# K and V in one load each, and the scores, P, b1 and wo that go with it, in a one-token attention and MLP kernel

## The chip, the core and the metric

The kernel runs on one core of a Trainium2 chip. A core has TensorE (PE, matmuls), VectorE (DVE), ScalarE (ACT), GpSimd (POOL), SyncE (SP, which here only issues transfers) and 16 DMA engines that carry all transfers between HBM and SBUF. The metric is the device time of one execution in microseconds; lower is better.

## The reference

One token of width 1024 goes through two branches that are added to it. The weights and the two caches, 39.85 MB in all, are read once.

```python
xn = layernorm(x)                                   # x: 1 x 1024
# A: attention of one token over the last W = 4096 keys
q = (xn @ wq).reshape(32, 128)                      # wq: 1024 x 4096; 32 heads
k, v = k_cache[:, -W:], v_cache[:, -W:]             # 4 groups x 4096 x 128, 8 heads share a group
p = softmax(q @ k.T * 128**-0.5)
a = (p @ v).reshape(4096) @ wo                      # wo: 4096 x 1024
# B: an MLP
y = layernorm(xn)
b = gelu(y @ w1 + b1) @ w2 + b2                     # w1: 1024 x 3584, w2: 3584 x 1024
out = x + a + b
```

## The kernel before

**Order.** Every engine runs one list of instructions, written out by hand, with semaphore waits between engines. What sets the order of the big transfers is SP's list, one queue: the first half of wq (rows 0 to 3 of 8 per partition), the first K load, the second half of wq, the second K load, all of W1; then, after a wait for the last K transpose (`C["kt", 3]`, since V overwrites K in the tile `KV`), two V loads (L313); after a wait for q's last matmul (`done["q"]`), W2 in 16 and 12 rows per partition (it overwrites wq in `BIG`); after a wait for W1's last matmul (`done["h"]`), wo in 8, 12, 9, 2 and 1 rows per partition (L320). Of wo, 20 rows go to `BIG` behind W2 and 12 to `KT`. x, b2 and b1 are loaded by ACT's queue at the start; b1 is laid out as 128 partitions of 28 numbers.

**K and V.** `pairs(cache, c)` describes one load, that of groups 2c and 2c+1 (L228). The memory side is walked as 64 rows m, within each 2 groups g, within each 64 keys of 128 numbers (16 KB that lie in one piece). On the SBUF side these are 128 partitions, so partition 2m + g holds 64 keys of one group and neighbouring partitions hold different groups:

```python
return cache[0, 2 * c:2 * c + 2, SK - W:SK, :].rearrange("g (m i) d -> m g (i d)", m=64)
```

**Attention.** DVE turns K in four transposes of 4096 columns (L285, `turn_k`, in blocks of 32 x 32), three of them ahead of q's own transpose and one behind. q (64 matmuls, weights streamed against a zero-padded x, `XZ`) is copied out, turned and spread into `QBD`. PE adds a mask into four PSUM banks (L455: -1e30 where a column's key belongs to the other group than the row's) and then 32 score matmuls of 512 columns. DVE takes two maxima, brings them together across partitions, ACT takes the exponential of 2048 columns with its sum, DVE turns P in one transpose into `PT` (L350), and after W1's product PE does 32 matmuls of `PT` with V (L433, two groups of 256 columns). DVE divides by the sum and picks each row's part, and four small matmuls (`pe_turn_o`, L513) turn the result. These are done after four of the W2 rounds.

**MLP and end.** W1's product is 56 matmuls into one bank; four small matmuls (L494) turn it, DVE adds b1 and does the GELU. W2 and the first 20 rows of wo are multiplied in 12 rounds of four rows (`pe_round`), each after POOL has raised `s_feed` for its rows' landing. The last 12 rows of wo are multiplied in four column strips of 32 PSUM partitions each as they land (L433, 128 x 256 pieces), ACT and DVE evict bank 7 (L400), SP writes the output as two rows of 512.

All matmuls that add into a bank go through the helper `add`, so they share line L433 in the profile and are told apart by their tiles: `BIG,XZ` is q, `KT,QBD` scores, `BIG,YZ` W1, `KV,KT` P times V, `BIG,GO` the rounds, `KT,GO` the last rows.

## Time and profile before

| | us |
|---|---|
| median of 3 runs | 99.3 (99.14 to 99.41) |
| the profiled execution | 99.2 |
| its span in the profile | 97.6 |
| PE, DVE, ACT, POOL busy | 71.6, 37.9, 8.1, 10.2 |
| DMA queue q1, share of 16 engines' span | 95.7% |
| K lands (second load), W1 lands, wo lands | 32.4, 49.3, 95.5 |
| last K transpose ends, V issued | 42.9, 42.9 |
| scores, W1's product, P times V end | 48.2, 62.1, 72.0 |

Times are from the span's start. A group's row gives line, engine, operation, tiles written and read, count; behind the first bar busy time and the mean of one in ns; behind the second the idle time of the engine just before and what ended it. In the chain, "DMA BIG<-in_B_w_dram 47%" is the share of the span in which the end waited for that transfer. Issue rows have KB per transfer and the median time from issue to landing; a transfer queued behind others has a long one. The slice rows give tenths busy in 40 equal slices of the span.

### The profile page before, as it was taken

How to read it: one execution, taken by the hardware profiler on the slowest of the kernel's cores; microseconds unless marked ns; L12 is line 12 of the kernel's file. 1: busy time of each engine (PE TensorE's matmuls, PEld its weight loads, DVE VectorE, ACT ScalarE, POOL GpSimd, SP SyncE). 2: the span in 40 equal slices, each digit the busy share in tenths (PEclk: the TensorE clock that was granted, in tenths of full speed). 3: DMA queues.
4: the chain of work that ended last, by engine and by line, in shares of the span. 5: the costliest groups of instructions: out<-in, count | busy, mean ns of one | idle time of the engine just before them, and what ended most of it. 6: DMA issues, size and time to landing. Idle time of an engine off the chain costs nothing.

```text
span 97.6 us, 1259 instructions
## 1 busy us (share of the span) xinstructions
PE 71.6 (73%) x337; PEld 30.1 (31%) x349; DVE 37.9 (39%) x50; ACT 8.1 (8%) x16; POOL 10.2 (10%) x29
## 2 busy tenths in 40 slices
PE   0005000399999973879979999799989999997991
PEld 0001000033444320323334444333344444443450
DVE  0001899899930699950581800050043000000001
ACT  0500000600000023000008000200000010000001
POOL 6999600000000000000000000000000000000000
PEclk9999999999999999999999999999999999999999
DMA  7599999999999998888999999999899998999980
GB/s 215 228 431 444 410 432 437 430 430 443 417 430 464 682 400 376 376 376 376 430 437 430 437 497 443 443 430 400 373 464 423 430 480 363 453 436 416 438 329 1
DMA packets 2229, 39.88 MB, mean 409 GB/s; under 512 B 434, under 2 KB 436, under 8 KB 692
## 3 DMA queue, kind: packets, MB, share of 16 engines
q1 hardware_dynamic: 2020, 39.85, 95.7%
q10 hardware_dynamic: 208, 0.01, 0.1%
q8 instruction: 1, 0.02, 0.1%
HBM read 39.86 MB, written 0.00 MB: 409 GB/s over the span
## 4 chain that ended last, share of the span: by engine, by line
DMA 79%; PE 13%; SPq 4%; issue 1%; DVE 0%
DMA BIG<-in_B_w_dram 47%; DMA KT<-in_A_wo_dram 32%; PE PS L433 13%; SPq L320 2%; SPq L232 1%; SPq L159 1%; DVE Pb L400 0%
## 5 line engine op out<-in xcount | busy, mean ns | idle before, releaser
L433 PE MATMUL PS<-BIG,GO 128*128 x84 | 20.1, 379 | 1.4 <-POOLq L419 0.5
L285 DVE STREAM_TRANSPOSE KT<-KV 128x4096 bf16<-128x4096 bf16 x4 | 17.6, 4432 | 4.8 <-DMA KV<-in_A_k_cache_dram 4.8
L433 PE MATMUL PS<-BIG,XZ 128*128 x64 | 16.2, 418 | 0.0
L433 PEld LDWEIGHTS PS<-BIG,GO 128*128 x96 | 9.3, 98 | 11.8 <-issue 1.7
L433 PE MATMUL PS<-BIG,YZ 128*128 x56 | 12.4, 380 | 0.7 <-DMA BIG<-in_B_w_dram 0.7
L433 PE MATMUL PS<-KT,QBD 128*128 x32 | 8.0, 379 | 2.6 <-DVE QBD L305 1.8
L433 PEld LDWEIGHTS PS<-BIG,XZ 128*128 x64 | 6.7, 105 | 9.9 <-issue 4.5
L400 DVE CAST Pb<-PS 64x256 bf16<-64x256 f32 x1 | 0.4, 417 | 21.7 <-PE PS L433 21.7
L433 PE MATMUL PS<-KV,KT 128*128 x32 | 8.3, 381 | 0.6
L430 PE MATMUL PS<-XBRP,HOT 1*128 1x512 bf16 x3 | 1.7, 620 | 9.0 <-DVE XZ L275 9.0
L433 PEld LDWEIGHTS PS<-BIG,YZ 128*128 x56 | 5.4, 96 | 7.5 <-issue 1.9
L426 PE MATMUL PS<-XBRP,onesb 1*128 1x512 bf16 x2 | 1.0, 605 | 8.2 <-DMA XBRP<-in_A_x_dram 8.2
L433 PEld LDWEIGHTS PS<-KT,QBD 128*128 x32 | 3.1, 96 | 7.5 <-issue 5.4
L245 DVE BATCH_NORM_STATS2 BN<-PS 128x6 f32<-128x512 f32 x2 | 1.3, 689 | 9.3 <-PE PS L426 9.3
L433 PEld LDWEIGHTS PS<-KV,KT 128*128 x32 | 3.1, 96 | 5.4 <-issue 3.9
L334 DVE TENSOR_REDUCE MX<-PS 128x1 f32<-128x1024 f32 x2 | 2.4, 1220 | 4.4 <-PE PS L433 4.4
L383 DVE SCALAR_TENSOR_TENSOR QBD<-PS,REC,HALF 32x256 f32<-32x256 f32 x2 | 0.9, 473 | 7.0 <-PE PS L433 6.9
L430 PEld LDWEIGHTS PS<-XBRP,HOT 1*128 1x128 bf16 x3 | 0.3, 118 | 10.2 <-DVE XZ L275 9.9
L350 DVE STREAM_TRANSPOSE KT<-Pb 128x2048 bf16<-128x2048 bf16 x1 | 2.3, 2312 | 2.1 <-ACT Pb L346 2.1
L356 DVE TENSOR_TENSOR HT<-PS,B1T 128x28 f32<-128x28 f32 x1 | 0.2, 209 | 7.4 <-PE PS L494 7.4
L346 ACT ACTIVATE Pb<-PS,NMB 128x2048 bf16<-128x2048 f32 x1 | 2.0, 1967 | 13.0 <-DVE NMB L343 13.0
L426 PEld LDWEIGHTS PS<-XBRP,onesb 1*128 1x128 bf16 x2 | 0.1, 98 | 8.2 <-issue 8.2
(76 smaller groups left out, 37.6 us busy)
## 6 DMA issues: line engine op xcount, KB each, us to landing
BIG<-in_A_wq_dram SPq DMA_DIRECT2D x2, 4096.0 KB, 18.9
BIG<-in_B_w_dram SPq DMA_DIRECT2D x1, 7168.0 KB, 46.0
KV<-in_A_k_cache_dram SPq DMA_DIRECT2D x2, 2048.0 KB, 23.2
KV<-in_A_v_cache_dram SPq DMA_DIRECT2D x2, 2048.0 KB, 13.4
BIG<-in_B_w_dram SPq DMA_DIRECT2D x1, 4096.0 KB, 24.6
BIG<-in_B_w_dram SPq DMA_DIRECT2D x1, 3072.0 KB, 31.2
BIG<-in_A_wo_dram SPq DMA_DIRECT2D x1, 3072.0 KB, 25.6
KT<-in_A_wo_dram SPq DMA_DIRECT2D x1, 2304.0 KB, 30.6
```

The costliest lines, as they stand in the source:

```text
L159: sp.dma_start(dst[:, c0 * width:(c0 + n) * width].rearrange("p (c n) -> p c n", c=n), src[:, c0:c0 + n, :],).then_inc(semaphores[j], 16)
L232: sp.dma_start(KV[:, c * 8192:(c + 1) * 8192], pairs(A_k_cache, c)).then_inc(s_k[c], 16)
L245: DVE.mark(dve.bn_stats(out=BN[:, 12 * n + 6 * i:12 * n + 6 * i + 6], in_=src[:, 512 * i:512 * i + 512]))
L285: C["kt", n] = DVE.mark(dve.transpose(KT[:, n * 4096:(n + 1) * 4096], KV[:, n * 4096:(n + 1) * 4096]))
L320: sp.dma_start(home[:, first:first + n * D], wo_flat[:, c0 * D:(c0 + n) * D]).then_inc(s_wo[j], 16)
L334: C["mx"] = DVE.mark(dve.tensor_reduce(out=MX2[:, n:n + 1], in_=S[:, 1024 * n:1024 * n + 1024], axis=AX.X, op=ALU.max))
L346: C["exp"] = ACT.mark(act.activation(out=Pb[:, :], in_=S, func=ACTF.Exp, bias=NMB[:, 0:1], scale=SCALE, accum_out=SUMP[:, 0:1]))
L350: C["d_pt"] = DVE.mark(dve.transpose(PT[:, 0:2048], Pb[:, :]))
L383: DVE.mark(dve.scalar_tensor_tensor(out=ONM.rearrange("p (i c d) -> p i c d", i=2, c=PAIRS)[:, i], in0=PS[rows, 512:1024].rearrange("p (c ...
L426: last = pe.matmul(bank(i), lhsT=onesb[0:1, :], rhs=XB[0:1, 8 * i:8 * i + 8, :])
L430: pe.matmul(bank(n), lhsT=HOT[:, 8:136], rhs=XB[0:1, 0:8, :], start=True, stop=False, skip_group_check=True)
L433: return pe.matmul(to, lhsT=lhsT, rhs=rhs, start=False, stop=False, skip_group_check=True, **place)
```

## The change

K comes in one load, behind wq's first half, and V in one load. The memory side is now walked as 4 groups g, within each 32 rows m, within each 128 keys of 128 numbers (32 KB in one piece), so that partition 32g + m holds keys of group g alone. All four K transposes follow that one landing, and q's transpose stands behind them. With one group per block of 32 partitions the scores need no mask: they go to two banks, 32 matmuls of 512 columns as before, the exponential covers 1024 columns. P is turned in four transposes of 32 partitions each into the diagonal blocks of `PT` (now 4096 columns, filled with zeros by POOL after the scores), and 32 matmuls with V follow, four groups of 128 columns. The maxima and the result are turned by DVE alone; the four matmuls of `pe_turn_o` and the branches around them are gone. The PSUM banks are started by three ACT copies of zeros instead of edge matmuls. b1 is loaded as 32 pieces of 112 numbers and is added by four small matmuls. wo comes in 16, 11, 4 and 1 rows; 16 go through rounds (11 rounds in all), 16 through the strips, and all stay in `BIG`.

```diff
-WO_CHUNKS = [8, 12, 9, 2, 1]
-WO_HEAD = 2
+WO_CHUNKS = [16, 11, 4, 1]
+WO_HEAD = 1
...
-TAIL = 20
+TAIL = 16
...
-ROUNDS = 12
-TURN = 4
+ROUNDS = 11
...
-PT = KT[:, 16384 - 2112:16384]
+PT = KT[:, 0:4096]
...
-    act.dma_start(B1T[:, :], B_b1.rearrange("(p c) -> p c", c=FC)).then_inc(s_b1, 16)
+    act.dma_start(B1R[:, :], B_b1.rearrange("(p c) -> p c", p=32)).then_inc(s_b1, 16)
...
-    def pairs(cache, c):
-        return cache[0, 2 * c:2 * c + 2, SK - W:SK, :].rearrange("g (m i) d -> m g (i d)", m=64)
-
-    def load_k(c):
-        sp.dma_start(KV[:, c * 8192:(c + 1) * 8192], pairs(A_k_cache, c)).then_inc(s_k[c], 16)
+    act.wait_ge(POOL.sem, C["QZ"])
+    for first in (0, 4):
+        ACT.mark(act.activation(out=PS[:, first * 512:(first + 2) * 512].rearrange("p (b n) -> p b n", b=2),
+                                in_=QZ[:, 0:512].unsqueeze(1).to_broadcast([128, 2, 512]), func=ACTF.Copy))
+    ACT.mark(act.activation(out=bank(7), in_=QZ[:, 0:512], func=ACTF.Copy))
+
+
+    def keys(cache):
+        return cache[0, :, SK - W:SK, :].rearrange("g (m i) d -> g m (i d)", m=32)
 
     load_chunks(WA, wq_p, WQ_CHUNKS[:1], NQ, s_wq)
-    load_k(0)
+    sp.dma_start(KV[:, :], keys(A_k_cache)).then_inc(s_k, 16)
     load_chunks(WA, wq_p, WQ_CHUNKS[1:], NQ, s_wq[1:], WQ_CHUNKS[0])
-    load_k(1)
     load_chunks(W1, w1_p, W1_CHUNKS, F, s_w1)
...
-    def turn_k(n):
-        dve.wait_ge(s_k[n // 2], 16)
-        C["kt", n] = DVE.mark(dve.transpose(KT[:, n * 4096:(n + 1) * 4096], KV[:, n * 4096:(n + 1) * 4096]))
-
-    for n in range(3):
-        turn_k(n)
...
+    dve.wait_ge(s_k, 16)
+    for n in range(4):
+        C["kt"] = DVE.mark(dve.transpose(KT[:, n * 4096:(n + 1) * 4096], KV[:, n * 4096:(n + 1) * 4096]))
...
-    sp.wait_ge(DVE.sem, C["kt", 3])
-    for c in range(PAIRS):
-        sp.dma_start(V[:, c * 8192:(c + 1) * 8192], pairs(A_v_cache, c)).then_inc(s_v, 16)
+    sp.wait_ge(DVE.sem, C["kt"])
+    sp.dma_start(V, keys(A_v_cache)).then_inc(s_v, 16)
...
     dve.wait_ge(ACT.sem, C["exp"])
-    C["d_pt"] = DVE.mark(dve.transpose(PT[:, 0:2048], Pb[:, :]))
+    dve.wait_ge(POOL.sem, C["consts"] + 1)
+    for g in range(4):
+        C["d_pt"] = DVE.mark(dve.transpose(
+            PT[32 * g:32 * g + 32, :].rearrange("p (i y) -> p i y", y=128)[:, :, 32 * g:32 * g + 32],
+            Pb[32 * g:32 * g + 32, 0:1024].rearrange("p (i m) -> p i m", m=32)))
...
-    pool.wait_ge(DVE.sem, C["kt", 1])
-    pool.sem_inc(s_feed, 1)
-    pool.wait_ge(DVE.sem, C["kt", 3])
-    pool.sem_inc(s_feed, 1)
+    pool.wait_ge(done["sc"], 4)
+    POOL.mark(pool.memset(PT, 0.0))
...
+    pe.wait_ge(s_b1, 16)
+    turned = PS[:, 2 * 512 + 32:2 * 512 + 64].rearrange("p (c t) -> p c t", c=4)[:, :, 0:7]
+    for q in range(4):
+        pe.matmul(turned, lhsT=E4[:, q * 128:(q + 1) * 128],
+                  rhs=B1R[:, q * FC:(q + 1) * FC].rearrange("p (t c) -> p c t", c=4),
+                  start=(q == 0), stop=False, skip_group_check=True)
...
-    for n in range(4):
-        pe.matmul(bank(3 + n), lhsT=OTHER[:, :], rhs=ALT[:, :], start=True, stop=False, skip_group_check=True)
...
+    with pe.Fori(0, 4) as t:
+        for e in range(4):
+            for n in range(2):
+                last = add(bank(4 + n), QZ[:, bass.ds(t * 8 + e * ZW, 128)],
+                           K3[:, bass.ds(t * -32 + (96 + 16 * n), 16), 32 * e:32 * e + 32])
+        last.then_inc(done["sc"], 1)
...
+    with pe.Fori(0, 4) as t:
+        for u in range(8):
+            last = add(bank(1), PT[:, bass.ds(t * 1024 + u * 128, 128)], V4[:, :, bass.ds(t * 1024 + u * 128, 128)])
+        last.then_inc(done["pv"], 1)
```

## The prediction

> **What bounds the kernel now.** I read the page first: busy shares, the slices, the chain that ended last.

> ```profile
> DMA  7599999999999998888999999999899998999980
> ...
> ## 4 chain that ended last, share of the span: by engine, by line
> DMA 79%; PE 13%; SPq 4%; issue 1%; DVE 0%
> DMA BIG<-in_B_w_dram 47%; DMA KT<-in_A_wo_dram 32%; PE PS L433 13%; SPq L320 2%; SPq L232 1%; SPq L159 1%; DVE Pb L400 0%
> ```
> The 16 DMA engines are busy in every slice from 5 us to the end, and the chain is transfers: W1 up to 49.3, then (behind 12.5 us of W1's matmuls, in which other transfers run) wo up to 95.5. The page's queue table says the same in bytes.

> ```profile
> DMA packets 2229, 39.88 MB, mean 409 GB/s; under 512 B 434, under 2 KB 436, under 8 KB 692
> q1 hardware_dynamic: 2020, 39.85, 95.7%
> q10 hardware_dynamic: 208, 0.01, 0.1%
> ```
> 39.85 MB in 95.7% of 16 x 97.6 us is 26.7 GB/s per engine. In the trace's packet records a 16 KB packet takes 0.611 us, 24 KB 0.912, 32 KB 1.213, 56 KB 2.116, 4 KB 0.159, 2 KB 0.084: 27.0 GB/s for the long ones, and the last 2 KB packets are no faster when most of the engines have stopped. So it is one engine's own rate, and the end of the stream is set by the engine with the most bytes. Now all have the same.

> The packet counts also tell how transfers are shared out. q1 has 14 loads of 128 pieces each; with one semaphore write from each of 16 engines that is 14 x 144 = 2016, and 4 are left: the output's two pieces and **two** semaphore writes. The page's 434 packets under 512 B agree: 160 small pieces of x, b2 and b1, 17 loads x 16 = 272 writes, and 2. A transfer cut in two runs on two engines; the others, whose outermost cut has 16, 64 or 128 pieces, run on all 16. Then the transfer queue's own waits, and of the groups and the issue rows two lines:

> ```profile
> SPq L313 <- DVE KT L285: 39.0, 1, 39.0
> SPq L320 <- PE PS L433: 16.9, 1, 16.9
> ```

> ```profile
> L285 DVE STREAM_TRANSPOSE KT<-KV 128x4096 bf16<-128x4096 bf16 x4 | 17.6, 4432 | 4.8 <-DMA KV<-in_A_k_cache_dram 4.8
> ...
> BIG<-in_B_w_dram SPq DMA_DIRECT2D x1, 7168.0 KB, 46.0
> ```
> The transposes follow K's landing and V's issue follows them. SP's waits of 39.0 and 16.9 us cost nothing: V is issued at 42.9 and W1 (46.0 us after its issue at 3.3) lands at 49.3, wo is issued at 62.2 and W2 lands at 76.0, so the engines never run dry.

> **The K and V loads: the term that decides.** Both are described anew. Before, a load's outermost cut is 64 rows (m), then 2 groups (g): 16 engines. After, it is 4 groups, then 32 rows of 32 KB. By the counts above I take it that a transfer is divided along its outermost cut, so K and V each run on four engines, 32 packets each. Per engine of these four: K 32 x 1.213 = 38.8 us and V 38.8, together 77.6, where the four K and V loads now cost every engine 32 x 0.611 = 19.6. That is **+58.1 us on these four**; the other twelve lose 19.6. In the same unit the rest is unchanged: wq 9.7 for each half, W1 8 x 2.116 = 16.9, W2 8 x (1.213 + 0.912) = 17.0; wo is 8 x (1.213 + 0.837 + 0.310 + 0.084) = 19.55 against 19.62 (0.837 and 0.310 lie between the neighbouring packet sizes).

> The four engines' queue, if it never runs dry: wq's first half lands at 12.9 as now, K 51.7, wq's second half 61.4, W1 78.3, V 117.1, W2 134.1, wo 153.5 (now 95.5, and 58.0 more). Does anything starve it? V waits at the SP queue for the last K transpose: 51.7 + 4 x 4.43 = 69.5, and 1.4 from issue to first packet (0.81 to 2.16 at the start), 70.9 before 78.3: 7 us in hand. Queued behind V on SP is W2, which waits for q: the second half of wq lands at 61.4, and 32 matmuls at 0.25 (16.2 us for 64) to 0.43 (the first ten after the idle start, 19.6 to 23.8) end at 69.5 to 75: long before 117. wo waits for h: q copied, turned and spread (0.6, 0.67, 0.7) at about 72 to 77, scores 8.0 to 85, W1's product 12.5 to 98: before 134. So the end is the sum.

> Everything after the last landing stays: four matmuls, the two evictions, the output. Now that is 97.6 - 95.5 = 2.1 us, and 99.2 - 97.6 = 1.6 outside the span. 99.2 + 58.0 = **157.2** in the profiled execution's terms, 0.1 more in the median's (99.3).

> [...] The output row alone fits two readings, "as many engines as outermost pieces" and "as many as pieces of any kind", for no transfer here has few outermost pieces and many in all. [...]

> **The rest of the change, all beside the stream.** PE drops three edge matmuls (0.62 each, two between x and q) and four mask matmuls (1.0), the four of o2 (0.26), and gains four small ones for b1 (0.2 each, like L494's); 32 score and 32 PV matmuls stay, same size. DVE: two constants more (each under L278's 0.58), one maximum of 1.22 for two, four small steps for nine, the exponential on 1024 columns (half of 1.97), four transposes of P of about 1.2 (between 0.67 for 512 columns and 2.31 for 2048) for one of 2.31, and five steps after PV for three. ACT gets three PSUM fills behind a wait for POOL's QZ, 2.8 us by L291's 0.60 per 512; queued behind them is the first square root at 11.0, and ACT idles 6.9 us before it. POOL loses eleven selects and fills (ALT's 2.30 the longest) and gains fills of QZ and MX at the start and of PT: 4096 columns at GO's 1.48 per 1664, 3.65 us. That fill waits for the scores, POOL's feed of W2 queues behind it, and DVE's P transposes wait for it; W1's product of 12.5 us covers all that (1.4 + 0.9 + 1.2 + 4.8 after the scores, or 3.65 + 4.8), and without this cover PV would start up to 3 us later. With V at 117 it waits for V anyway. b1 in 32 pieces: 96 packets fewer in a queue of 0.1%, nothing; PE's wait for it now stands ahead of the scores, but it lands 14.6 us after an issue at 2.1.

> **The tail** is the one place where PE may add. wo's 16 rows land at 143.7; until then PE idles from 139 (W2's second chunk at 134.1, 24 matmuls at 0.214) for 4.6 us. Now, 9 us idle was followed by ten matmuls at 0.427 and 1.8 us idle by none. If slow: 32 matmuls take 6.9 + 2.1, the 11 rows 1.5, the rest 0.9, ending about 154.9 instead of 153.8. Between 0 and 1.1; I take 0.4, nearer to no slowdown by the length of the idle. **157.7 us.**

> **Rivals.** *All 16 engines share K and V* (the second reading, and the other side). Then K's 128 packets spread as now, at 32 KB: 16 x 1.213 instead of 32 x 0.611 saves 0.14, wo 0.06, three transfers fewer 0.03: 99.07, no change that can be told. For it: the SBUF side of the transfer still has 128 rows. Against: no transfer in the trace is shared out over two cuts at once. It decides at once whether K lands at 12.9 + 9.7 = 22.6 or at 51.7. K at 22.6 puts the transposes' end at 40.4; q's second half waits for wq at 32.3, ends by 40.4 to 42.5; scores by 50 to 52, W1's product by 62.5 to 65, W2's rounds by 84 to 87 against wo's landing at 85.8. PE would then just keep up.

> *K on four engines, V on four others.* Then V starts when it is issued, 70.9, ends at 109.7, and W2 and wo behind it end at 146.3: 150.0 us. For it: nothing in the trace shows which engines the two of the output are. Against: both loads look alike.

> *The four run slower.* Four streams start 16 MB apart, which no load does now. At the 25.8 GB/s of the 4 KB packets instead of 27.0, K and V take 3.6 us more: with the tail's 1.1, 162. [...]

> **How the numbers follow.** Four engines for both: 0.80, and 157.7, since all 18 transfers counted fit the outermost cut and the other reading needs a sharing over two cuts that none shows. V elsewhere: 0.05. Slower than 162: 0.04. All 16: 0.11, of which a third may be measurably faster (over 0.3%, 0.3 us, which is about what a measurement of this kernel can tell), half the same, the rest slower. Slower in all: 0.80 + 0.05 + 0.04 + 0.02 = 0.91. The range of 8 in 10 runs from the 150 of V elsewhere to 162 and holds 0.85; the 99 is left out.

> **What would show it.** K landing near 52 and W1 near 78; a DMA slice row at 2 or 3 tenths from some 40 us (the twelve have wq and W1 by 12.9 + 9.7 + 16.9) until W2's issue near 72, and again from about 120 to the end; 1564 packets on q1 (nine loads of 144, two of 132, the output's 4) instead of 1588, and K's and V's bytes moving at 4 x 27 = 108 GB/s; DVE idle for some 32 us before the first K transpose; PV's start at V's landing, about 117. Wrong: K landed at 23, a DMA row of nines, a chain that ends as now. Half right: V landing near 110, or a DMA gap before V.

## The result, and the profile after

The changed kernel takes 274.37 us, the median of 6 runs (270.85 to 280.22); the kernel before takes 99.2 (6 runs, 99.12 to 99.41). The ratio is 2.752, 95% interval 2.736 to 2.768; it leaves out the two longest runs. The profiled execution took 274.85 us with a span of 273.4.

The page of the changed kernel, the rows that answer to those shown of before:

```profile
DMA  8999998999322222222999999999989422222110
GB/s 307 395 206 216 198 206 174 198 173 139 64 58 53 53 67 93 103 107 85 331 187 216 185 233 163 149 158 145 160 129 154 93 82 80 111 104 108 82 52 21
DMA packets 1678, 39.88 MB, mean 146 GB/s; under 512 B 267, under 2 KB 269, under 8 KB 397
...
q1 hardware_dynamic: 1564, 39.85, 66.6%
q10 hardware_dynamic: 112, 0.01, 0.0%
...
## 4 chain that ended last, share of the span: by engine, by line
another core or an unknown queue 81%; PE 11%; DMA 5%; POOL 1%; issue 1%; DVE 0%; ACT 0%; POOLq 0%
...
L264 DVE STREAM_TRANSPOSE KT<-KV 128x4096 bf16<-128x4096 bf16 x4 | 17.4, 4413 | 90.7 <-DMA KV<-in_A_k_cache_dram 90.7
L401 PE MATMUL PS<-KV,KT 128*128 x32 | 8.9, 446 | 80.2 <-DMA KV<-in_A_v_cache_dram 80.2
...
BIG<-in_B_w_dram SPq DMA_DIRECT2D x1, 7168.0 KB, 134.7
KV<-in_A_k_cache_dram SPq DMA_DIRECT2D x1, 4096.0 KB
KV<-in_A_v_cache_dram SPq DMA_DIRECT2D x1, 4096.0 KB
```

Two rows of the page of before, for comparison (its DMA row and its row of the K transposes stand in the prediction):

```profile
GB/s 215 228 431 444 410 432 437 430 430 443 417 430 464 682 400 376 376 376 376 430 437 430 437 497 443 443 430 400 373 464 423 430 480 363 453 436 416 438 329 1
...
L433 PE MATMUL PS<-KV,KT 128*128 x32 | 8.3, 381 | 0.6
```

- The count on q1 is 1564: nine loads of 144, two of 128 + 4, the output's 4. K and V ran on **four engines each**. K's semaphore shows it too: one write right after the issue (at 2.3) and four more as data land (99.8 to 109.8), where a load on all engines has 16. It goes with this that the chain's 81% has no name and that K's and V's issue rows have no landing time.
- DVE waits 90.7 us for K (4.8 before) and PE 80.2 for V (0.6 idle ahead of that group before).
- The slices at 2 tenths, about 4 of 16 engines, are there. But their rate is 53 to 64 GB/s from 68 to 96 us, half of what four engines at 27 would move; and with all engines busy, from 14 us on, it is about 200 where before it was 400 to 440 in most slices.

The stretches, in the answer on windows (us; busy time of each engine; granted TensorE clock; DMA share; GB/s). The window rows of the experiments have the same columns:

```profile
core 0: us, PE busy (x) PEld busy (x) DVE busy (x) ACT busy (x) POOL busy (x), PEclk, DMA share, GB/s
14.00:32.00 18.00, 8.88 (x32) 3.58 (x32) 4.74 (x11) 1.69 (x3) 0.00 (x0) 1.00 1.04 202
78.00:97.00 19.00, 0.00 (x0) 0.00 (x0) 0.00 (x0) 0.00 (x0) 0.00 (x0) 0.50 0.26 57
110.00:117.00 7.00, 0.00 (x0) 0.00 (x0) 7.00 (x2) 0.00 (x0) 0.00 (x0) 0.50 0.24 105
131.00:135.00 4.00, 2.84 (x8) 1.12 (x8) 0.52 (x3) 0.50 (x2) 0.00 (x0) 0.66 0.97 362
...
168.00:184.00 16.00, 0.00 (x0) 0.00 (x0) 0.00 (x0) 0.00 (x0) 0.00 (x0) 0.50 1.01 152
```

At 78 to 97 only K's four engines run: 57 GB/s, 14 for each. At 110 to 117 the same four carry their share of wq and W1: 105, or 26 each. So these engines are not slow; **K is slow on them**. At 14 to 32 (K beside wq) and 168 to 184 (V beside wo) all 16 are busy, and all are slow. The trace's packet records say it piece by piece (before, a 32 KB packet takes 1.21 us, a 56 KB one 2.12). They carry no engine's number; packets are put in one row where one starts as the other ends:

```
what                               us            one packet, us
K, two of the four engines         13 to 53      2.5       (32 KB)
                                   53 to 74      3.3 to 3.9
                                   74 to 99      2.2 to 2.6
K, the other two                   13 to 74      3.1 to 3.9, most 3.8 (32 KB)
                                   74 to 109     2.2 to 2.6, every fourth 1.5 to 2.0
wq, W1 on the other twelve,        13 to 54      2.5 to 2.6 (32 KB), 4.3 to 5.0 (56 KB)
  all but one
one of them, three in turn         13 to 53      3.0 to 3.8 (32 KB), 5.1 to 6.7 (56 KB)
all twelve                         54 to 72      6.1 to 6.8 (56 KB)
wq, W1 on the four, after K        99 to 136     1.21      (32 KB), 2.12 (56 KB)
```

K lands at 109.8 (forecast 51.7), W1 at 137.2 (78.3), V at 234.1 (117.1), the last row of wo at 270.5. What waits for K and V starts right behind, and V's issue follows the last transpose:

```profile
L401 PE MATMUL PS<-KV,KT x32: 379/379/634, 234.4 to 242.9; 128*128 x32
L264 DVE STREAM_TRANSPOSE KT<-KV x4: 4402/4402/4445, 109.8 to 122.8; 128x4096 bf16<-128x4096 bf16 x4
...
L284 SPq DMA_DIRECT2D KV<-in_A_v_cache_dram x1: 577/577/577, 127.3 to 127.3; - x1
```

### The profile page after: what moved, and what is told of

It reads as the page before. It is cut to its first block, busy times and chain, and to the rows that moved or that the text cites. A ratio compares the mean times of both kernels' runs of the same rounds, so it can differ in the third digit from the quotient of the medians.

```text
span 273.4 us, 1221 instructions
## 1 busy us (share of the span) xinstructions
PE 73.5 (27%) x339; PEld 31.5 (12%) x350; DVE 40.9 (15%) x48; ACT 10.8 (4%) x19; POOL 9.3 (3%) x21
## 2 busy tenths in 40 slices
DMA packets 1678, 39.88 MB, mean 146 GB/s; under 512 B 267, under 2 KB 269, under 8 KB 397
## 3 DMA queue, kind: packets, MB, share of 16 engines
q1 hardware_dynamic: 1564, 39.85, 66.6%
## 4 chain that ended last, share of the span: by engine, by line
another core or an unknown queue 81%; PE 11%; DMA 5%; POOL 1%; issue 1%; DVE 0%; ACT 0%; POOLq 0%
PE PS L401 11%; DMA BIG<-in_A_wq_dram 5%; POOL KT L385 1%; DVE Pb L269 0%; ACT Pb L267 0%; ACT QZ L280 0%; DVE Pb L374 0%; POOLq L391 0%; POOLq L383 0%; POOLq L381 0%
## 5 line engine op out<-in xcount | busy, mean ns | idle before, releaser
L401 PE MATMUL PS<-BIG,XZ 128*128 x64 | 18.6, 462 | 102.1 <-POOLq L383 91.9
L264 DVE STREAM_TRANSPOSE KT<-KV 128x4096 bf16<-128x4096 bf16 x4 | 17.4, 4413 | 90.7 <-DMA KV<-in_A_k_cache_dram 90.7
L401 PE MATMUL PS<-KV,KT 128*128 x32 | 8.9, 446 | 80.2 <-DMA KV<-in_A_v_cache_dram 80.2
L401 PE MATMUL PS<-BIG,GO 128*128 (+1 forms) x141 | 22.7, 344 | 5.6 <-POOLq L391 4.9
L401 PEld LDWEIGHTS PS<-BIG,GO 128*128 (+1 forms) x152 | 10.6, 100 | 18.0 <-issue 11.1
L401 PE MATMUL PS<-KT,QZ 128*128 x32 | 8.8, 442 | 1.2 <-ACT QZ L280 1.2
L385 POOL MEMSET KT<- 128x4096 bf16 x1 | 3.5, 3517 | 134.4 <-PE PS L401 134.4
L322 DVE STREAM_TRANSPOSE KT<-Pb 32x1024 bf16<-32x1024 bf16 x4 | 4.9, 1236 | 1.4 <-ACT Pb L316 1.3
L401 PEld LDWEIGHTS PS<-KT,QZ 128*128 x32 | 3.6, 111 | 6.4 <-issue 3.7
L304 DVE TENSOR_REDUCE MX<-PS 128x1 f32<-128x1024 f32 x1 | 1.2, 1224 | 9.5 <-PE PS L401 9.5
L202 ACT ACTIVATE PS<-QZ 128x1024 f32<-128x1024 bf16 x2 | 2.0, 1018 | 0.0
L243 DVE TENSOR_REDUCE XNT<-Pb 128x8 f32<-128x1024 bf16 x1 | 1.9, 1945 | 0.0
## 6 DMA issues: line engine op xcount, KB each, us to landing
BIG<-in_B_w_dram SPq DMA_DIRECT2D x1, 7168.0 KB, 134.7
```

What stands on the lines that cost most here:

```text
L202: ACT.mark(act.activation(out=PS[:, first * 512:(first + 2) * 512].rearrange("p (b n) -> p b n", b=2), in_=QZ[:, 0:512].unsqueeze(1).to_br ...
L243: DVE.mark(dve.tensor_reduce(out=XNT[:, :], in_=XM.rearrange("p (a r) -> p r a", r=KC), axis=AX.X, op=ALU.add))
L264: C["kt"] = DVE.mark(dve.transpose(KT[:, n * 4096:(n + 1) * 4096], KV[:, n * 4096:(n + 1) * 4096]))
L304: DVE.mark(dve.tensor_reduce(out=MX[:, 0:1], in_=S, axis=AX.X, op=ALU.max))
L322: C["d_pt"] = DVE.mark(dve.transpose(PT[32 * g:32 * g + 32, :].rearrange("p (i y) -> p i y", y=128)[:, :, 32 * g:32 * g + 32], Pb[32 * g:3 ...
L385: POOL.mark(pool.memset(PT, 0.0))
```

## Experiments

Kernels 1 to 7 are the changed kernel with an edit, the eighth is the kernel before with one. Experiment 2 was run 12 times, the others once; the changed kernel's own six runs lie between 270.85 and 280.22. Two theories of the author's stand against each other in them. A, the memory side: four streams that read in step, 16 MB apart, hold each other up. B, the SBUF side: engines that write partitions 32 apart in step share one engine's rate. That they share it two by two, in two pairs, is an estimate from the packets: twice 1.213 us is 2.43, near the 2.5 in the table above, and four to a rate would take 4.85. Why the loads of before, over 128 partitions, show no such sharing (1.213 us per 32 KB packet) B does not say: no record tells which partitions an engine writes.

**1. The distance in HBM.** The four groups' reads start 16 MB less 36 KB apart instead of 16 MB (other keys are read, so the attention result is not the reference's).

```
 def keys(cache):
-    return cache[0, :, SK - W:SK, :].rearrange("g (m i) d -> g m (i d)", m=32)
+    pitch, size = SK * DH - 144 * DH, W * DH
+    flat = cache.rearrange("b g s d -> (b g s d)")
+    return flat[0:4 * pitch].rearrange("(g x) -> g x", g=4)[:, 0:size].rearrange("g (m y) -> g m y", m=32)
```

> The change, but the four groups' reads of K and of V start 16 MB less 36 KB apart instead of exactly 16 MB (other keys are read, so the output is not the reference's). In the changed kernel's trace a 32 KB packet of the four engines takes about 2.5 us instead of 1.213, and the other twelve engines' packets are slow too. Theory A, memory side: four streams that run in step exactly 16 MB apart collide in HBM. Then this run falls to the forecast's 157.7 us, with 32 KB packets at 1.2 us. [...]

278.59 us. Two rows of its page:

```profile
DMA  7999997999322222222999999999999412222210
...
L266 DVE STREAM_TRANSPOSE KT<-KV 128x4096 bf16<-128x4096 bf16 x4 | 17.4, 4414 | 91.6 <-DMA KV<-in_A_k_cache_dram 91.6
```

DVE waits 91.6 us for K, as long as in the changed kernel (90.7), and the time lies among that kernel's own (B: no change, about 274 us). The distance of exactly 16 MB is not the cause.

**2. Everything but the cut.** The same two loads, with 32 rows outermost instead of 4 groups.

```
-        return ....rearrange("g (m i) d -> g m (i d)", m=32)
+        return ....rearrange("g (m i) d -> m g (i d)", m=32)
```

> The change, but the memory side of K and V is walked rows m first, groups second (32 outermost pieces), so that 16 engines share each load; the rows land on other partitions, so the output is not the reference's. Both theories: the time of all the rest of the change, 99.1 us (98.9 to 99.6) by the forecast's sum for 16 engines. If it is well above 100, the rest of the change (PE's, DVE's or POOL's steps) costs what the sum put at nothing.

99.05 us, ratio to before 1.0007 (0.9983 to 1.0031).

```profile
DMA  7799999999999988888999999998899999899880
...
q1 hardware_dynamic: 1588, 39.85, 95.5%
...
L264 DVE STREAM_TRANSPOSE KT<-KV 128x4096 bf16<-128x4096 bf16 x4 | 17.4, 4413 | 3.6 <-DMA KV<-in_A_k_cache_dram 3.6
```

1588 is eleven loads of 144 and the output's 4: all 16 engines. K landed at 22.5 us. One permutation of the outer two dimensions carries the whole loss; all the rest of the change (no mask, block-diagonal P, b1, wo's cut) is worth nothing that can be told.

**3. All 16 engines on 32 partitions.** Four loads per cache, each of one group into 32 partitions.

```
+    def load(cache, semaphore):
+        for g in range(4):
+            sp.dma_start(KV[32 * g:32 * g + 32, :], keys(cache)[g]).then_inc(semaphore, 16)
```

> The change, but K and V come in four loads each, one per group, into the same partitions; each has 32 outermost pieces and runs on 16 engines, two packets each. Theory A: no two groups are read in step, full rate, 99.3 us. [...]

121.25 us. Windows: K, then wq's second half with the start of W1, then V:

```profile
13.00:31.00 18.00, 8.72 (x32) 3.52 (x32) 5.54 (x12) 1.69 (x3) 0.00 (x0) 1.00 0.99 204
35.00:41.00 6.00, 0.00 (x0) 0.00 (x0) 6.00 (x2) 0.00 (x0) 0.00 (x0) 0.50 0.98 421
62.00:78.00 16.00, 12.33 (x61) 5.61 (x59) 9.89 (x17) 2.02 (x4) 3.23 (x1) 0.97 0.95 197
```

204 and 197 GB/s with all 16 engines busy, 421 between. Half the rate without any transfer on four engines and with no two groups read in step, where A has the full rate: loads into 32 neighbouring partitions suffice for it. With half the rate K and V take 9.7 us more each, 99.3 + 19.4 = 118.7 us, B's figure. The packets take 2.57 us, not twice 1.213; 16 of them on each engine, 0.14 longer each, are 2.2 of the 2.5 us above it.

**4. Four engines on blocks 24 apart.** 96 partitions in blocks of 24, four engines; the last 32 in a load of their own on eight.

```
+    def load(cache, semaphore):
+        sp.dma_start(KV[0:96, :], keys(cache)[:, 0:24]).then_inc(semaphore, 16)
+        sp.dma_start(KV[96:128, :], keys(cache)[:, 24:32].rearrange("g m y -> m g y")).then_inc(semaphore, 16)
```

> The change, but of each load 24 of 32 rows per group go to partitions 0 to 95 (four groups outermost, exactly 16 MB apart, four engines), whose blocks start 24 apart; the other 8 rows of each group come in a second load with rows first (8 engines, 4 packets each). The output is not the reference's, since rows land on other partitions. Theory A: the four are as slow as in the change for 24 of 32 packets: K and V take about 72 us each instead of 96, 235 us. [...]

216.1 us, away from both figures: A's 235, and B's 148 with every packet at 1.213 us (12.9 + 2 x (29.1 + 4.9) + 9.7 + 16.9 + 17.0 + 19.6 = 144.1, and 3.7 after it).

```profile
34.00:62.00 28.00, 0.00 (x0) 0.00 (x0) 0.00 (x0) 0.00 (x0) 0.00 (x0) 0.50 1.00 211
74.00:84.00 10.00, 0.00 (x0) 0.00 (x0) 6.94 (x2) 0.00 (x0) 0.00 (x0) 0.50 0.28 120
```

While the other twelve engines run, all 32 KB packets take 2.2 to 2.58 us; from about 68, when the four are alone, 1.22. The four no longer hit one another, but they are slow while other engines write wq, W1 or wo. The theory of pairs alone was incomplete, and what it lacks is with the other twelve's traffic. One reading, the author's, is that **one of the other twelve counts as a writer too** where it shares with one of the four; this run does not show it by itself, since here all 16 engines slow down alike. Experiment 8 and the changed kernel's packets, where one engine after another is hit harder than the rest, go with it.

**5. Pairs, with nobody else.** The changed kernel; SP waits for each of the two loads before it issues more.

```
     sp.dma_start(KV[:, :], keys(A_k_cache)).then_inc(s_k, 16)
+    sp.wait_ge(s_k, 16)
...
     sp.dma_start(V, keys(A_v_cache)).then_inc(s_v, 16)
+    sp.wait_ge(s_v, 16)
```

> The change, but SP issues nothing between K's load and its landing, nor between V's load and its landing, so that the four engines of K and V run without the other twelve's traffic (those twelve stand idle meanwhile). [...] Alone only the pair is left: every K and V packet 2.43 us, 77.8 us a load instead of 96 and 97. 12.9 + 77.8 + 26.6 (second half of wq, W1) + 77.8 + 17.0 + 19.6, with some 4 for two restarts of the stream and 3.7 after it: about 239 us. If the others' traffic is not what lengthens the packets: K and V stay at 96 and 97, and idling the twelve only adds: about 280.

235.25 us, **less** than the changed kernel, though twelve engines now stand idle behind each load.

```profile
14.00:84.00 70.00, 9.25 (x32) 3.70 (x32) 4.57 (x11) 1.69 (x3) 0.00 (x0) 0.64 0.25 57
90.00:113.00 23.00, 11.67 (x41) 4.56 (x42) 15.43 (x7) 1.10 (x3) 0.00 (x0) 0.65 0.98 425
118.00:185.00 67.00, 15.53 (x76) 7.04 (x73) 10.20 (x17) 2.02 (x4) 3.52 (x1) 0.64 0.25 55
```

K takes 73.8 us (13.1 to 86.9) and V 76.8 (115.9 to 192.7) at 57 and 55 GB/s, where 38.8 each was forecast. Most packets take 2.4 to 2.6 us; of each engine's, every fourth takes 1.5 to 2.3, as if the two of a pair, a little out of step, did not hit one another for a part of every fourth packet. This is the price of the pairs by themselves.

**6. Neither pairs nor others.** The edits of 4 and 5 together.

> e4's loads (four engines on blocks 24 apart for 24 of 32 rows, 8 engines for the rest; the output is not the reference's) with the waits of e5_alone. [...] If four engines on one load are slow by themselves (reads 16 MB apart, or a limit per load): 2.4 us a packet, about 210.

152.73 us; B's figure, with packets at 1.213 us, is 152 (12.9 + 2 x (29.1 + 4.9) + 26.6 + 17.0 + 19.6 = 144.1, 4 for two restarts of the stream and 3.7 after it).

```profile
14.00:40.00 26.00, 8.75 (x32) 3.51 (x32) 4.64 (x11) 1.69 (x3) 0.00 (x0) 0.86 0.27 116
76.00:100.00 24.00, 14.87 (x73) 6.76 (x70) 10.20 (x17) 2.02 (x4) 3.52 (x1) 0.88 0.29 126
```

At a DMA share of 0.27 to 0.29 the engines move 116 and 126 GB/s, 27 each, with reads from four places 16 MB apart, and most of K's and V's 32 KB packets take 1.213 us. Four engines at their full rate is what the prediction had assumed; they have it on blocks 24 apart with the other engines idle.

**7. K alone so cut.** V with its rows outermost.

```
-    sp.dma_start(V, keys(A_v_cache)).then_inc(s_v, 16)
+    sp.dma_start(V, keys(A_v_cache).rearrange("g m y -> m g y")).then_inc(s_v, 16)
```

> The change for K; V's load is walked rows first (16 engines; rows land on other partitions, so the output is not the reference's). If the price is each load's own: K takes 96 us as in the change, V 9.7: 12.9 + 96.1 + 9.7 + 16.9 + 9.7 + 17.0 + 19.6 with 3.7 after it = 185.6 us. If the loss comes from somewhere else behind K's landing (PE's clock, the later rounds), it stays well above 190.

185.1 us: half of the loss, with the stretch of 2 tenths there once.

```profile
DMA  6999999999995992322221222223999999999910
...
q1 hardware_dynamic: 1576, 39.85, 72.5%
```

**8. One stray writer in the kernel before.** A load on a single engine (17 rows) beside the ordinary ones. It fetches data that nothing uses. In the changed kernel and in experiments 3 and 4 the packets of all 16 engines were long together (2.2 to 2.6 us and more per 32 KB); here one engine is to show whether that spreads.

```
+    sp.dma_start(KT[64:81, 12288:16384], A_wq.rearrange("(p r) n -> p (r n)", r=KC)[64:81, 0:4096]).then_inc(s_stray, 16)
...
+    dve.wait_ge(s_stray, 16)          # ahead of turn_k(3)
```

> The kernel before, with one extra load behind K's first: 17 rows of 8 KB from wq into a free part of KT on partitions 64 to 80 (17 is divisible by no number up to 16 but 1, so one engine should do all of it). [...] Coupled: during this load (some 10 us from about 18) every engine's 32 KB packets take about 2.4 us. Local: only the engines whose partitions these are slow down, the others stay at 1.21. In both the end is set by the engine with the extra rows: 99.2 + 17 x 0.62 = 109.7 us, or 104.5 if it isn't slowed either.

2038 packets on q1, 18 more than before: 17 rows and one semaphore write, so it is one engine. 108.58 us lies between the two figures, but the time decides nothing, for it holds what the expectation left out: the last K transposes waited for this engine's part of K, V was issued at 54.0 instead of 42.9, and the engines were nearly dry from 48 to 55 us.

```profile
DMA  6899999999799998992049999999999999999920
...
13.00:17.00 4.00, 0.00 (x0) 0.00 (x0) 3.97 (x4) 0.00 (x0) 0.00 (x0) 1.00 0.98 415
21.00:27.00 6.00, 6.00 (x20) 2.26 (x19) 6.00 (x2) 0.00 (x0) 0.00 (x0) 1.00 1.02 362
33.00:48.00 15.00, 9.39 (x33) 3.79 (x34) 4.62 (x2) 0.60 (x1) 0.00 (x0) 0.69 1.02 440
```

The packets say more. Of the stray's 17 packets of 8 KB 12 take 0.61 to 0.69 us instead of 0.31 (the shortest 8 KB packets of the changed kernel), and three 0.39 to 0.41. Five other engines, one after another, take 1.5 to 2.55 per 32 KB; that the stray's rows meet these five in turn is the author's reading, as the records name no engine. **All the others go from 1.21 to 1.33 to 1.45** between 20 and 28 us. (They stay at 1.21 until 20, when the stray's packets have been long for 2 us, and are back at it once the stray has ended.) So neither "coupled" nor "local" holds as it was put: the one stray engine slows five others most and the rest by some 15%; with the changed kernel's four it was a factor of two.

## Why the prediction was right or wrong

**Right: how many engines.** Four each for K and V, read from the output's two semaphore writes. 1564 packets, and experiment 2's 1588 and full rate with the other order, leave nothing of the rival "all 16". Nor does "V on four others" fit: two engines begin with V at 128.6, when the other twelve are idle, and two more only at 135.0 and 136.2, as W1 ends on the slower two of K's four.

**Right: what is hidden.** V was issued at 127.3, 9.9 us before W1 landed at 137.2 (7 us in hand were forecast): the slower two of the four, which set the end, never ran dry. The faster two had ended W1 at 125.8 and stood idle until 128.6.

```profile
SPq L284 <- DVE KT L264: 124.3, 1, 124.3
SPq L375 <- DVE Pb L374: 105.5, 1, 105.5
SPq L291 <- PE PS L401: 22.7, 1, 22.7
```

These waits of SP are the longest in the changed kernel, and V's, of 124.3 us, costs nothing, as the one of 39.0 did before; the second, of 105.5, is the output's wait for the end. Experiment 2 shows the same of all the PE, DVE, ACT and POOL work, forecast at 0.1 us less than before and measured at a ratio of 1.0007. The tail is 2.9 us from the last landing to the end instead of 2.1: 0.8 where 0.4 was taken between 0 and 1.1.

**Wrong: the duration of a packet.** The forecast was 157.7 us. The step that failed is "so it is one engine's own rate", carried over to a load that spreads over the partitions in another way, and with it the term 32 x 1.213 = 38.8 us per load. It measured 96.7 (K, from 13.1 to 109.8) and 96.9 (V, 137.2 to 234.1), 3.0 us per packet. That an engine alone has 1.213 us is right, as experiment 6 shows; what the term lacked is that engines that write partitions 32 apart share a rate (experiment 5 against 6: mostly 2.4 to 2.6 us per 32 KB packet against 1.213). The 27.0 GB/s were read from loads over 128 partitions, where every engine had them; one engine's limit and a limit that two engines share elsewhere could not be told apart there. The last 2 KB packets, no faster with most engines stopped (0.084 us), excluded a limit common to all, not one shared by two. The sum with the measured sizes:

- 99.2 + 58.0 for the four engines' 64 packets at their own rate: 157.2
- the pairs' sharing, from experiment 5: 73.8 + 76.8 - 77.6 = 73.0
- the other twelve engines' traffic, the changed kernel against experiment 5: 96.7 + 96.9 - 73.8 - 76.8 = 43.0

273.2, against the profiled execution's 274.85; the 0.8 of the tail is half of the rest. Everything late in the list of landings follows from this one duration.

The third rival, **the four run slower**, had the direction and the wrong cause and size: a loss of 3.6 us to four streams 16 MB apart. Experiment 1 shows no gain without the 16 MB (278.59 us), experiment 6 no loss with them (packets at 1.213 us); a pattern with more engines at such a pitch was not run.

**Which engine meets which.** The trace has no numbers of engines or partitions, so this was not shown. The packet records have two durations beside the other twelve's traffic, 2.5 us for two of the four and mostly 3.8 for the other two, and the step of the faster two to 3.3 to 3.9 at 53 us, after just 16 packets. By multiples of 1.213, an estimate, 2.43 is two to a rate and 3.64 three: the third would be one of the twelve, and with those idle K's 32 packets take 73.8 us, 2.3 each (experiment 5). The records also have three of the twelve hit harder one after another (13.8 to 28.7, 26.8 to 45.4, 40.9 to 53.0: 3.0 to 3.8 us per 32 KB where the rest have 2.5 to 2.6).

**Open:** why the other engines are held back as well. Experiment 8 shows that it happens (1.33 to 1.45 us instead of 1.21), and beside the changed kernel (2.5 to 2.6) that it is more with four such writers than with one; no run here shows by what. The twelve end at 214 to 217 us, well before V, so how much they lose does not set the end; how much of the 43.0 is such spreading and how much a third writer was not told apart.

## What to carry to other kernels

Read a load's outermost dimension twice: here it set how many engines ran (four with 4 groups outermost, 16 with 32 rows: 1564 and 1588 packets on q1), and how the destination's partitions were dealt to them; with four blocks of 32 partitions both went wrong, and swapping two dimensions of the same access pattern gave back 175 us (the rows then land on other partitions, and the steps that use them have to follow). A packet's duration is the price of the whole pattern (the engine, the partitions that others write in step, the traffic beside it: 1.21 to 3.9 us for 32 KB here), so carry it to a changed load only if that load spreads over the destination as the measured one does. When a slice shows few DMA engines busy, divide its GB/s by that many: here 26 each meant that they were few, 14 each that they also collided.
